# HGRN recurrence and a capacity-limited mixture of experts on one core: the second product of an expert in one matmul per chunk, one block of zeros moved, the scatters re-spaced

## The chip, the cores and the metric

The kernel runs on one core of a Trainium2 chip. The metric is the device time of one launch in microseconds (us), as the median of three runs. All times "at" some moment are counted from the start of the profiled span.

## What is computed

First a recurrence over time is run on 4 sequences of 5056 steps with 256 channels each; its output, 20224 rows of 256 numbers, goes into a router with 8 experts. An expert keeps at most 80 rows, those with the highest gate weight, and every other row of the output is zero.

```python
sig = 1 / (1 + exp(-f_logit))
f = lower_bound + (1 - lower_bound) * sig
for t in range(S):                      # S = 5056, h is (4, 256)
    h = f[:, t] * h + (1 - f[:, t]) * x[:, t]
    y[:, t] = h
...
expert = argmax(x @ w_gate)             # x is y as 20224 rows of 256
for e in range(8):                      # capacity 80 rows
    hid = maximum(x[tok] @ w1[e], 0)    # 256 -> 1024
    out[tok] = gate[tok, None] * (hid @ w2[e])   # 1024 -> 256
```

Everything is float32. The inputs of the recurrence are 41 MB, the weights of the experts 17 MB, the output 21 MB.

## The kernel before, in words

The kernel has three stages.

**Load stage.** A unit is 512 time steps of one sequence; there are 40. For each unit `load` brings in `f_logit` and `x` (512 KB each), ScalarE and GpSimd form the gate and the input, TensorE turns both so that time lies along the free axis (L251, L259), VectorE scans (L276), and TensorE computes the router's logits (L289). SyncE issues all loads on one queue, in program order. The output's zeros are written on the same queue, in blocks of 512 KB: `copied` (L137) copies a block that is already zero from one place of the output to another, `clear` (L151) writes one from a tile of zeros. One block goes out after every fourth unit's loads.

**Selection.** A short stage of VectorE, TensorE and GpSimd work picks the rows of each expert. In it the first 7 halves of weights and 22 blocks of zeros are put in the queue.

**Expert stage** (`experts`). Weights come in 32 halves of 512 KB, numbered 0 to 31 in the order of `halves_of`: both halves of `w1` of expert 0, then for each expert e both halves of `w1[e+1]` and both halves of `w2[e]`. They live in a ring of 7 slots, so half k is issued when half k - 7 has been used up. `more` issues two halves, and behind half k as many `copied` blocks as the tuple `BETWEEN` names k. Halves 20 and 21 are `w2` of expert 4, 24 and 25 of expert 5, 30 and 31 of expert 7; the last half is loaded in two pieces.

For expert e, `gather` copies its 80 columns one by one out of `h_all` (24 by VectorE, 32 by ScalarE, 24 by GpSimd), and `scaled` multiplies them. `hidden` computes the first product: 32 matmuls with 64 columns of weights each, two of them side by side in the array, 80 columns moving. `relu` turns it into `hid`, the first four chunks by ScalarE, the other four by VectorE. `result` computes the second product: for each of 8 chunks of 128 hidden units, `hid` is the stationary operand and 256 columns of `w2` move. A chunk is done as two matmuls, for slots 0 to 63 and for slots 64 to 79:

```python
H = P // 2
...
for c in range(FC):
    for s0, n in ((0, H), (H, K - H)):
        marks[e, c] = nc.tensor.matmul(
            y[ds(s0, n)], hid[:, c, ds(s0, n)], halves[c // CH][:, c % CH],
```

`finish` multiplies by the gates on VectorE, and `scatter` sends the 80 rows to the output with one indirect DMA from GpSimd's queue. TensorE's order is hidden(0), hidden(1), result(0), hidden(2), result(1), and so on to hidden(7), result(6), result(7). The scatters stand behind the gathers in GpSimd's program; `apart` names for a scatter the matmul (expert, chunk) whose end it waits for; the last scatter waits for all others to land.

Of the kernel before, what the change touches and what calls it, by code (L numbers as in the profile page):

```python
# [26 lines left out]
def kernel(  # L27
# [11 lines left out]
    nc = tc.nc  # L39
    B, S, D = x.shape  # L40
    E, _, F = w1.shape
    N = B * S
    DC = D // P
    FC = F // P
# [5 lines left out]
    K = (capacity + TOP - 1) // TOP * TOP  # L50
# [20 lines left out]
    FH, CH = F // 2, FC // 2  # L71
# [13 lines left out]
    def slot(i, name):  # L85
        return ring[i].tile([P, R * D], F32, name=name, tag="buf")
# [44 lines left out]
    def copied():  # L131

        at = written[0]
        n = min(P * ZH, TOTAL - at)
        if n:
            z = 2 * ZH if n % (2 * ZH) == 0 else D
            nc.sync.dma_start(out=out_flat[ds(at, n)].rearrange("(p k) -> p k", k=z),  # L137
                              in_=out_flat[:n].rearrange("(p k) -> p k", k=z))
            written[0] += n

    def clear(source):

        n = source.shape[1]
        at = written[0]
        if at >= TOTAL:
            return
        rows = min(P, (TOTAL - at) // n)
        if rows == 0:
            rows, n = 1, TOTAL - at
        dst = out_flat[ds(at, rows * n)].rearrange("(p k) -> p k", p=rows)  # L150
        nc.sync.dma_start(out=dst, in_=source[:rows, :n])  # L151
        written[0] += rows * n
# [9 lines left out]
    with tc.tile_pool(name="gsm", bufs=1) as gsm:  # L162
# [49 lines left out]
        def small_loads():  # L212

            nc.sync.dma_start(out=small[:, :E * P],
                              in_=w_gate.rearrange("(o p) e -> o (p e)", p=P))
            nc.sync.dma_start(out=small[:, E * P:], in_=lower_bound.rearrange("(o p) -> o p", p=P))

        def small_turned():
            turn = plt.tile([P, E + 1, DC], F32, name="small_t", tag="lt")
            for e in range(E + 1):  # L220
                row = small[:, e:E * P:E] if e < E else small[:, E * P:]
                nc.tensor.transpose(turn[:, e], row, ident[:DC, :DC])
            nc.vector.tensor_scalar(nomlb, turn[:, E], 1.0, -1.0, ALU.mult, ALU.add)
            nc.vector.tensor_scalar(omlb, turn[:, E], -1.0, 1.0, ALU.mult, ALU.add)
            return turn
# [158 lines left out]
        def unit(f, m):  # L384
            if 0 <= m < n_unit:
                f(m)
# [11 lines left out]
        TURN = LAST * B  # L398
# [3 lines left out]
        with tc.tile_pool(name="plg", bufs=1, space=PSUM) as plg, \  # L402
             tc.tile_pool(name="plt", bufs=1, space=PSUM) as plt:
            with tc.tile_pool(name="pss", bufs=2, space=PSUM) as pss, \
                 tc.tile_pool(name="psu", bufs=3, space=PSUM) as psu:
                for n in range(-AHEAD, n_unit):
                    unit(load, n + AHEAD)
                    m = n + AHEAD
                    if m == 1:
                        small_loads()  # L410
                    if m == 3:
                        clear(early)
                    elif 3 < m < TURN and m % 4 == 3:
                        copied()
                    elif m == n_unit - 1:
                        for _ in range(3):
                            copied()
                    unit(gate, n + 2)
                    if n == -2:
                        turn = small_turned()  # L420
                    if n == -1:
                        scaled_gate(turn)
                    unit(enter, n + 2)
                    unit(turn_s, n + 1)
                    unit(turn_u, n + 1)
                    if n == n_unit - 2:
                        zbuf = slot(0, "zbuf")
                        nc.gpsimd.memset(zbuf, 0.0)
                        exponentials(0, LAST - 1)
                    unit(decay, n + 1)  # L430
                    unit(scan, n)
                    if n > 1 and n % B == 1:
                        aside(n // B - 1)
                    if n == n_unit - 3:
                        assert len(jobs) == 4
                    some_of(1 if n < TURN or n >= n_unit - 3 else 2 if n < n_unit - 1 else 0)
                    if n == n_unit - 2:
                        exponentials(LAST - 1, LAST)
                        summed(0, 4)
                        valued(0, 4, nc.gpsimd)  # L440
                    unit(logits, n - 1)
                    if n > 0 and n % B == 0:
                        g = n // B - 1
                        jobs.append(lambda g=g: by_token(g))
                        if g % 2 or g >= LAST - 1:
                            g0 = g - 1 if g < LAST - 1 else g
                            jobs += [lambda g0=g0, g=g: shifted(g0, g + 1),
                                     lambda g0=g0, g=g: equals(g0, g + 1),
                                     lambda g0=g0, g=g: choice(
                                         g0, g + 1, nc.gpsimd if g < LAST - 1 else nc.vector)]  # L450
            with tc.tile_pool(name="pct", bufs=4, space=PSUM) as pct:
# [32 lines left out]
                c = turn((6, LAST - 1), (LAST - 1, LAST))  # L484
# [38 lines left out]

    w_sb = {}
    RANKING = 12
    BETWEEN = (7, 8, 8, 10, 12, 13, 15, 16, 18)
    for k, key in enumerate(halves_of[:NSLOT - 1]):
        w_sb[key] = half(*key)
        copied()
# [68 lines left out]
    with tc.tile_pool(name="sel", bufs=1) as sel, \  # L598
# [17 lines left out]
        for r in (rivals2, rivals):  # L616
            nc.tensor.matmul(r, mates, spread.rearrange("p c k -> p (c k)"),
                             start=True, stop=True)
# [89 lines left out]
    def experts(again):  # L708
        with tc.tile_pool(name="xp", bufs=3) as xp, \
# [7 lines left out]
            sent, marks = [], {}  # L717
# [16 lines left out]
            H = P // 2  # L734
# [22 lines left out]
            def result(e):  # L757
                halves = [w.pop((2, e, i)) for i in range(2)]
                hid = HID.pop(e)
                y = Y[e] = psy.tile([K, D], F32, name="y_ps", tag="y_ps")  # L760
                for c in range(FC):
                    for s0, n in ((0, H), (H, K - H)):
                        marks[e, c] = nc.tensor.matmul(  # L763
                            y[ds(s0, n)], hid[:, c, ds(s0, n)], halves[c // CH][:, c % CH],
                            start=c == 0, stop=c == FC - 1, skip_group_check=True)

            def finish(e):
                if e == 0:
# [4 lines left out]
            def scatter(e, behind=None):  # L773

                sent.append(nc.gpsimd.indirect_dma_start(  # L775
                    out=out, out_offset=bass.IndirectOffsetOnAxis(ap=goal[:, ds(e, 1)], axis=0),
                    in_=rows.pop(e), in_offset=None, bounds_check=N - 1, oob_is_err=False))
                if behind:
                    tc.add_manual_dep(sent[-1].ins, marks[behind].ins.name, mybir.DependencyInfo(
                        mybir.DependencyClass.Sync, mybir.DependencyReason.DATA), reason="apart")  # L780
                for other in sent[:-1]:
                    if e < E - 1:
                        tc.declare_no_dep(sent[-1].ins, other.ins, reason="other rows")
                    else:
                        tc.add_manual_dep(sent[-1].ins, other.ins.name, mybir.DependencyInfo(
                            mybir.DependencyClass.Sync, mybir.DependencyReason.DATA),
                            reason="all rows")

            def more(m):
                for _ in range(2 * m):  # L790
                    if late:
# [3 lines left out]
                        if not again:  # L795
                            for _ in range(BETWEEN.count(k)):
                                copied()
# [13 lines left out]
            if not again:  # L811
                busy(psy, 3, "y_ps")

            apart = {2: (E - 3, FC - 1), 3: (E - 2, 0), 4: (E - 2, FC - 1), 5: (E - 1, 1),
                     6: (E - 1, FC - 2)}
            for e in range(E):
                relu(e, ps)
                if e == 0 and not again:
                    gates_of(slots[:, 1])
                if e + 1 < E:  # L820
                    ps = hidden(e + 1)
                    more(1)
                if e == E - 4:
                    scatter(0)
                if e + 3 < E:
                    gather(e + 3)
                    scaled(e + 3)
                if e == E - 4:
                    scatter(1)
                result(e)  # L830
                more(1)
                finish(e)
                if e == 0 and not again:
                    found = consts.tile([1, 1], F32, name="found")
                    nc.vector.tensor_reduce(found, total, AX.X, ALU.add)
                    nc.vector.tensor_copy(doubt, found)
                    rows_of(consts, slots[:, 0], slots[:, 1])
            for e in range(2, E):
                scatter(e, apart.get(e))

    experts(False)
    assert written[0] == TOTAL, written

# [88 lines left out]
```

## Time and profile before

| | |
|---|---|
| median of 3 runs | 252.69 us (252.64 to 252.92) |
| the profiled execution | 253.41 us |
| its span, first to last instruction | 251.5 us |
| TensorE busy | 221.4 us (88%) |
| VectorE / ScalarE / GpSimd busy | 156.8 / 133.1 / 143.2 us |
| bytes moved by DMA | 80.61 MB |
| second product (L763), matmul records and busy time | 256, 71.3 us |

A float32 matmul leaves two matmul records and two weight-load records in the profile, one pair for each of its two passes. Such records overlap, so a record's own duration is not what it costs; the distance from one start to the next is. Weight loads have rows of their own (PEld). A DMA's time "to landing" runs from its issue until its semaphore has its full count.

### The profile page before, as it was taken

Reading aid. Unit: us, or ns where it says so; the run is one execution under the profiler, and the core shown is the slowest. Engines: PE = TensorE matmul, PEld = TensorE weight load, DVE = VectorE, ACT = ScalarE, POOL = GpSimd, SP = SyncE. Lnnn points to the kernel's source line nnn. Section 1 sums busy time; section 2 is a strip of 40 time slices with the busy share of each in tenths; the row PEclk is TensorE's granted clock in tenths of the full one; section 3 lists DMA queues with packets and bytes.
Section 4 is the critical chain, followed back from the end, with each engine's and each line's share of the span. In section 5 each row is a group of like instructions: output and inputs, shape, how many; then the busy total and the mean of one; then the engine's idle time right before and its main releaser. Section 6 shows DMA issues by size and latency. Waiting matters only on the chain.

```text
span 251.5 us, 6853 instructions
## 1 busy us (share of the span) xinstructions
PE 221.4 (88%) x2223; PEld 141.9 (56%) x2223; DVE 156.8 (62%) x400; ACT 133.1 (53%) x419; POOL 143.2 (57%) x287
## 2 busy tenths in 40 slices
PE   0699899899989998999966899799999999999960
PEld 0698787778868787777834646252525344352210
DVE  4189699999999999899999567435415051010100
ACT  4488798779787886888826066755042300000000
POOL 4678797889788798779844067650450620011211
PEclk9999999999999999999997979999999999999996
DMA  6999999999999999999999999969985474620000
GB/s 248 377 410 449 371 425 412 418 420 401 412 405 408 397 434 391 395 403 412 400 363 417 416 444 402 417 257 345 340 300 199 154 250 137 219 95 14 26 20 17
DMA packets 21363, 80.61 MB, mean 320 GB/s; under 512 B 2580, under 2 KB 2710, under 8 KB 20888
## 3 DMA queue, kind: packets, MB, share of 16 engines
q1 hardware_dynamic: 20936, 79.45, 80.4%
q0 software_dynamic: 384, 0.66, 0.9%
q8 instruction: 19, 0.31, 0.5%
q14 instruction: 24, 0.20, 0.2%
HBM read 72.62 MB, written 21.36 MB: 374 GB/s over the span
## 4 chain that ended last, share of the span: by engine, by line
PE 45%; issue 19%; ACT 10%; DVE 9%; DMA 9%; POOL 4%; ACTq 1%; DVEq 0%; POOLq 0%; SPq 0%
PE y_ps L763 14%; PE sp L251 11%; PE up L259 9%; PE lg L289 6%; DMA x_t<-in_x_dram 5%; ACT h_all L268 4%; ACT xe L727 3%; PE h_ps L747 3%; DMA f_t<-in_f_logit_dram 3%; DVE h_all L276 3%; POOL out_dram L775 2%; PE lt L313 2%; POOL x_t L245 2%; ACT ls L298 2%; DMA out_dram<-y,goal 1%
## 5 line engine op out<-in xcount | busy, mean ns | idle before, releaser
L245 POOL TENSOR_TENSOR x_t<-f_t,x_t 128x1024 f32<-128x1024 f32 x40 | 94.7, 2370 | 21.1 <-DMA x_t<-in_x_dram 10.6
L276 DVE TENSOR_TENSOR_SCAN h_all<-h_all,up 128x512 f32<-128x512 f32 (+1 forms) x80 | 95.8, 1244 | 9.9 <-PE up L259 6.4
L763 PE MATMUL y_ps<-w_sb,hid 128*64 128x256 f32 (+1 forms) x256 | 71.3, 393 | 1.4 <-ACT hid L754 1.4
L268 ACT ACTIVATE h_all<-sp,nomlb 128x512 f32<-128x512 f32 (+1 forms) x80 | 50.3, 677 | 16.5 <-PE sp L251 15.7
L763 PEld LDWEIGHTS y_ps<-w_sb,hid 128*64 128x64 f32 (+1 forms) x256 | 19.4, 115 | 50.4 <-issue 48.8
L241 ACT ACTIVATE f_t<-f_t 128x1024 f32<-128x1024 f32 x40 | 42.3, 1058 | 9.8 <-DMA f_t<-in_f_logit_dram 7.3
L259 PE MATMUL up<-ident,x_t 128*128 128x128 f32 x320 | 44.0, 278 | 2.8 <-DVE h_all L276 2.2
L251 PE MATMUL sp<-ident,f_t 128*128 128x128 f32 x320 | 45.4, 287 | 0.0
L251 PEld LDWEIGHTS sp<-ident,f_t 128*128 128x128 f32 x320 | 35.9, 145 | 7.8 <-issue 7.1
L259 PEld LDWEIGHTS up<-ident,x_t 128*128 128x128 f32 x320 | 36.7, 143 | 5.1 <-DVE h_all L276 3.7
L771 DVE TENSOR_SCALAR y<-y_ps,gates 80x256 f32<-80x256 f32 x8 | 3.8, 480 | 57.0 <-PE y_ps L763 51.5
L727 ACT COPY xe<-h_all 128x2 f32 x256 | 25.4, 190 | 18.8 <-issue 12.2
L727 POOL COPY xe<-h_all 128x2 f32 x192 | 24.3, 189 | 14.2 <-issue 7.0
L727 DVE COPY xe<-h_all 128x2 f32 x192 | 22.7, 173 | 12.0 <-issue 7.4
L775 POOL DMA_INDIRECT out_dram<-y,goal x8 | 7.5, 942 | 35.3 <-PE y_ps L763 31.1
L289 PE MATMUL lg<-h_all,wg 128*32 128x128 f32 (+1 forms) x640 | 26.4, 282 | 0.6 <-ACT ls L298 0.6
L754 ACT ACTIVATE hid<-h_ps 128x320 f32<-128x320 f32 x8 | 3.5, 435 | 39.2 <-PE h_ps L747 21.3
L747 PEld LDWEIGHTS h_ps<-xe,w_sb 128*64 128x64 f32 x512 | 18.2, 138 | 4.1 <-issue 3.6
L747 PE MATMUL h_ps<-xe,w_sb 128*64 128x80 f32 x512 | 19.5, 234 | 0.0
L289 PEld LDWEIGHTS lg<-h_all,wg 128*32 128x32 f32 x640 | 15.4, 108 | 7.0 <-issue 4.9
L731 POOL TENSOR_TENSOR xe<-xe,omlb 128x160 f32<-128x160 f32 x8 | 3.6, 452 | 23.5 <-DVE xe L727 22.1
L160 PE MATMUL warm<-h_all,ident 128*128 128x512 f32 x22 | 13.1, 740 | 0.0
(128 smaller groups left out, 105.6 us busy)
## 6 DMA issues: line engine op xcount, KB each, us to landing
f_t<-in_f_logit_dram SPq DMA_DIRECT2D x40, 512.0 KB, 6.6
x_t<-in_x_dram SPq DMA_DIRECT2D x40, 512.0 KB, 6.9
w_sb<-in_moe_w_dram SPq DMA_DIRECT2D x31, 512.0 KB, 5.0
out_dram<-out_dram SPq DMA_DIRECT2D x26, 512.0 KB, 8.2
out_dram<-zbuf SPq DMA_DIRECT2D x12, 512.0 KB, 10.0
out_dram<-h_all SPq DMA_DIRECT2D x1, 512.0 KB, 8.2
w_sb<-in_moe_w_dram SPq DMA_DIRECT2D x2, 256.0 KB, 2.8
out_dram<-out_dram SPq DMA_DIRECT2D x1, 256.0 KB
```

Source lines behind the costliest of these rows:

```text
L160: nc.tensor.matmul(warm, ident, h_all[:, 0, :4 * P], start=True, stop=True)
L241: nc.scalar.activation(s_t, s_t, ACT.Sigmoid, scale=-1.0)
L245: nc.gpsimd.tensor_tensor(u_t, sts[n], u_t, ALU.mult)
L251: nc.tensor.transpose(ps[:, ds(r * P, P)], sts[n][:, r, ds(o * P, P)], ident)
L259: nc.tensor.transpose(ps[:, r::R], uts[n][:, r, ds(o * P, P)], ident)
L268: nc.scalar.activation(columns(n, o).rearrange("p (k r) -> p k r", r=R), sps.pop((n, o)).rearrange("p (r k) -> p k r", r=R)[:, P - run(n / ...
L276: nc.vector.tensor_tensor_scan(h, h, ups.pop((n, o)), h_all[:, o, ds(spot(n - B) + G - 1, 1)] if n >= B else 0.0, ALU.mult, ALU.add)
L289: nc.tensor.matmul(lgs[g][ds(q * LC, LC), b, :k].rearrange("p (m i) -> p m i", i=2), wg[:, o], pairs[:, :, q], start=o == 0, stop=o == DC ...
L727: copy(X[e][:, :, ds(k + j, 1)], h_all[:, :, ds(v, 1)])
L747: nc.tensor.matmul(ps[i][ds(s * H, H), c], wo[o][:, at:at + J * (H - 1) + 1:J], xt[:, o], start=o == 0 and c == 0, stop=o == DC - 1, skip_ ...
L763: marks[e, c] = nc.tensor.matmul(y[ds(s0, n)], hid[:, c, ds(s0, n)], halves[c // CH][:, c % CH], start=c == 0, stop=c == FC - 1, skip_grou ...
L775: sent.append(nc.gpsimd.indirect_dma_start(out=out, out_offset=bass.IndirectOffsetOnAxis(ap=goal[:, ds(e, 1)], axis=0), in_=rows.pop(e), i ...
```

## The change

The second product is one matmul per chunk, with all 80 slots as the stationary operand. The block of zeros behind the loads of unit 35 is left out, and `BETWEEN` has ten places instead of nine, with later numbers. The first scatter is issued behind the last gather instead of ahead of it; scatter 1 joins the loop at the end; and `apart` names other matmuls.

```diff
@@ -410,7 +410,7 @@
                         small_loads()
                     if m == 3:
                         clear(early)
-                    elif 3 < m < TURN and m % 4 == 3:
+                    elif 3 < m < TURN - 1 and m % 4 == 3:
                         copied()
                     elif m == n_unit - 1:
                         for _ in range(3):
@@ -523,7 +523,7 @@
 
     w_sb = {}
     RANKING = 12
-    BETWEEN = (7, 8, 8, 10, 12, 13, 15, 16, 18)
+    BETWEEN = (7, 8, 8, 9, 10, 12, 14, 17, 19, 21)
     for k, key in enumerate(halves_of[:NSLOT - 1]):
         w_sb[key] = half(*key)
         copied()
@@ -759,10 +759,9 @@
                 hid = HID.pop(e)
                 y = Y[e] = psy.tile([K, D], F32, name="y_ps", tag="y_ps")
                 for c in range(FC):
-                    for s0, n in ((0, H), (H, K - H)):
-                        marks[e, c] = nc.tensor.matmul(
-                            y[ds(s0, n)], hid[:, c, ds(s0, n)], halves[c // CH][:, c % CH],
-                            start=c == 0, stop=c == FC - 1, skip_group_check=True)
+                    marks[e, c] = nc.tensor.matmul(
+                        y, hid[:, c], halves[c // CH][:, c % CH],
+                        start=c == 0, stop=c == FC - 1, skip_group_check=True)
 
             def finish(e):
                 if e == 0:
@@ -811,8 +810,8 @@
             if not again:
                 busy(psy, 3, "y_ps")
 
-            apart = {2: (E - 3, FC - 1), 3: (E - 2, 0), 4: (E - 2, FC - 1), 5: (E - 1, 1),
-                     6: (E - 1, FC - 2)}
+            apart = {1: (E - 3, FC - 1), 2: (E - 2, 0), 3: (E - 2, CH), 4: (E - 2, FC - 1),
+                     5: (E - 1, 2), 6: (E - 1, FC - 2)}
             for e in range(E):
                 relu(e, ps)
                 if e == 0 and not again:
@@ -820,13 +819,11 @@
                 if e + 1 < E:
                     ps = hidden(e + 1)
                     more(1)
-                if e == E - 4:
-                    scatter(0)
                 if e + 3 < E:
                     gather(e + 3)
                     scaled(e + 3)
                 if e == E - 4:
-                    scatter(1)
+                    scatter(0)
                 result(e)
                 more(1)
                 finish(e)
@@ -835,7 +832,7 @@
                     nc.vector.tensor_reduce(found, total, AX.X, ALU.add)
                     nc.vector.tensor_copy(doubt, found)
                     rows_of(consts, slots[:, 0], slots[:, 1])
-            for e in range(2, E):
+            for e in range(1, E):
                 scatter(e, apart.get(e))
 
     experts(False)
```

On TensorE, in the expert stage, the rows before, from the first product of expert 1 (`h_ps`) into the second product of expert 0 (`y_ps`); the last two columns are stationary and moving columns:

```order
L747 MATMUL h_ps<-xe,w_sb 64x80 x32
L763 MATMUL y_ps<-w_sb,hid 64x256
L763 MATMUL y_ps<-w_sb,hid 16x256
L763 MATMUL y_ps<-w_sb,hid 64x256
L763 MATMUL y_ps<-w_sb,hid 16x256
```

and the same place of the change, on to the next expert:

```order
L747 MATMUL h_ps<-xe,w_sb 64x80 x32
L762 MATMUL y_ps<-w_sb,hid 80x256 x8
L747 MATMUL h_ps<-xe,w_sb 64x80 x32
L762 MATMUL y_ps<-w_sb,hid 80x256 x8
L747 MATMUL h_ps<-xe,w_sb 64x80 x32
```

Sixteen matmuls of an expert, alternating between 64 and 16 columns, have become eight of 80.

On SyncE's queue, in the expert stage before, from half 13 (`w2` of expert 2, its second) to half 21 (L514 is a half of `w1`, L520 a half of `w2`, L137 a block of zeros, the last one of 256 KB):

```order
L520 DMA w_sb<-in_moe_w_dram 128x2x512
L137 DMA out_dram<-out_dram 16x8192
L514 DMA w_sb<-in_moe_w_dram 128x1024 x2
L137 DMA out_dram<-out_dram 16x8192
L520 DMA w_sb<-in_moe_w_dram 128x2x512
L137 DMA out_dram<-out_dram 16x8192
L520 DMA w_sb<-in_moe_w_dram 128x2x512
L514 DMA w_sb<-in_moe_w_dram 128x1024
L137 DMA out_dram<-out_dram 16x4096
L514 DMA w_sb<-in_moe_w_dram 128x1024
L520 DMA w_sb<-in_moe_w_dram 128x2x512 x2
```

and of the change, from half 13 to half 23:

```order
L520 DMA w_sb<-in_moe_w_dram 128x2x512
L514 DMA w_sb<-in_moe_w_dram 128x1024
L137 DMA out_dram<-out_dram 16x8192
L514 DMA w_sb<-in_moe_w_dram 128x1024
L520 DMA w_sb<-in_moe_w_dram 128x2x512 x2
L137 DMA out_dram<-out_dram 16x8192
L514 DMA w_sb<-in_moe_w_dram 128x1024 x2
L137 DMA out_dram<-out_dram 16x8192
L520 DMA w_sb<-in_moe_w_dram 128x2x512 x2
L137 DMA out_dram<-out_dram 16x4096
L514 DMA w_sb<-in_moe_w_dram 128x1024 x2
```

The last block of zeros stood behind half 18 and stands behind half 21.

## Rows read from the trace of the kernel before

**Rows 1.** The page's slices (40, of 6.29 us each): DMA rate; then all bytes.
```profile
GB/s 248 377 410 449 371 425 412 418 420 401 412 405 408 397 434 391 395 403 412 400 363 417 416 444 402 417 257 345 340 300 199 154 250 137 219 95 14 26 20 17
DMA packets 21363, 80.61 MB, mean 320 GB/s; under 512 B 2580, under 2 KB 2710, under 8 KB 20888
```

**Rows 2.** Windows: PE, PEld, DVE, ACT, POOL busy (instructions); clock, DMA share, GB/s.
```profile
5.00:25.00 20.00, 16.70 (x157) 15.25 (x161) 12.49 (x15) 14.01 (x19) 14.44 (x7) 1.00 1.04 410
...
145.00:163.00 18.00, 16.57 (x159) 8.54 (x158) 11.54 (x95) 12.48 (x127) 13.12 (x96) 0.92 1.03 419
163.00:190.00 27.00, 27.00 (x219) 10.81 (x220) 9.63 (x67) 11.04 (x103) 10.39 (x76) 1.00 0.82 300
190.00:222.00 32.00, 32.00 (x281) 13.38 (x278) 7.96 (x54) 4.54 (x35) 5.95 (x28) 1.00 0.59 203
```

**Rows 3.** TensorE in order of time, expert stage: start, duration, instruction.
```profile
158.49 0.43 PE L763 MATMUL y_ps<-w_sb,hid 128*64 128x256 f32 x1 [1.43 <-ACT hid L754]
...
189.61 2.44 PE L747 MATMUL h_ps<-xe,w_sb 128*64 128x80 f32 x64
191.87 8.91 PE L763 MATMUL y_ps<-w_sb,hid 128*64 128x256 f32 x32
200.72 2.44 PE L747 MATMUL h_ps<-xe,w_sb 128*64 128x80 f32 x64
...
225.21 17.80 PE L763 MATMUL y_ps<-w_sb,hid 128*64 128x256 f32 x64
```

**Rows 4.** SyncE's queue: what issues waited for; us in total, times, longest.
```profile
SPq L520 <- PE y_ps L763: 23.4, 6, 4.0
SPq L514 <- PE y_ps L763: 18.1, 5, 4.5
```

**Rows 5.** TensorE's weight loads in order of time, within one second product.
```profile
192.40 0.11 PEld L763 LDWEIGHTS y_ps<-w_sb,hid 128*16 128x16 f32 x2 [0.39 <-issue]
192.93 0.19 PEld L763 LDWEIGHTS y_ps<-w_sb,hid 128*64 128x64 f32 x2 [0.42 <-issue]
193.51 0.11 PEld L763 LDWEIGHTS y_ps<-w_sb,hid 128*16 128x16 f32 x2 [0.38 <-issue]
```

**Rows 6.** The chain of waits in the load stage: eight transposes of one unit.
```profile
77.44 0.87 PE up L259 x8
```

**Rows 7.** Weight loads of these transposes, by shape: busy us, mean ns, idle before.
```profile
L259 PEld LDWEIGHTS up<-ident,x_t 128*128 128x128 f32 x320 | 36.7, 143 | 5.1 <-DVE h_all L276 3.7 <-POOL x_t L245 1.3
```

**Rows 8.** All DMA from 0 to 163 us.
```profile
DMA packets 16026, 65.43 MB, mean 401 GB/s; under 512 B 1980, under 2 KB 1982, under 8 KB 15666
```

**Rows 9.** The scatters' queue, from 163 us: packets, MB, share of 16 engines.
```profile
q0 software_dynamic: 384, 0.66, 2.5%
```

**Rows 10.** DMA issues of weights, 192 to 222 us: median us to landing.
```profile
w_sb<-in_moe_w_dram SPq DMA_DIRECT2D x9, 512.0 KB, 3.3
```

**Rows 11.** The same, 145 to 163 us.
```profile
w_sb<-in_moe_w_dram SPq DMA_DIRECT2D x5, 512.0 KB, 9.3
```

**Rows 12.** The chain of waits at the end: start, duration, what.
```profile
241.94 0.03 POOLq L775
...
242.18 3.13 DMA out_dram<-y,goal
```

**Rows 13.** ScalarE in order of time: two gathers, with a relu between.
```profile
160.03 3.34 ACT L727 COPY xe<-h_all 128x2 f32 x32 [1.59 <-issue]
...
165.36 3.12 ACT L727 COPY xe<-h_all 128x2 f32 x32 [1.67 <-issue]
```

**Rows 14.** VectorE in order of time: finish of expert 6, relu of expert 7.
```profile
234.16 0.48 DVE L771 TENSOR_SCALAR y<-y_ps,gates 80x256 f32<-80x256 f32 x1 [10.23 <-PE y_ps L763]
234.56 0.48 DVE L755 TENSOR_SCALAR hid<-h_ps 128x320 f32<-128x320 f32 x1
```

**Rows 15.** TensorE in order of time, where its clock fell.
```profile
134.00 1.22 PE L617 MATMUL rivals<-spread,mates 128*128 128x192 f32 x3 [2.65 <-DVE spread L611]
```

**Rows 16.** The window behind it, columns as in rows 2.
```profile
134.10:137.40 3.30, 3.30 (x7) 2.23 (x8) 3.26 (x8) 2.33 (x9) 1.88 (x8) 0.50 1.03 421
```

## The prediction

> **What bounds the kernel now.** I read the page's slices first. From the second slice to the 26th (6 to 163 us) DMA moves 363 to 449 GB/s, and then the rate falls off [rows 1]. The windows say the same by stage: 410 GB/s early in the loads, 419 from 145 to 163 us with all sixteen DMA engines busy, then 300 and 203 [rows 2]. What ends where DMA slackens is seen in the same windows: from 163 us TensorE is busy for 27.00 us of 27 and 32.00 of 32. So there are two regimes: the queue is full until about 160 us, and from the first second product, at 158.49 us, TensorE sets the time. SyncE's queue shows who waits: loads of weights wait 23.4 and 18.1 us in total for a second product to give a ring slot free [rows 4].
>
> TensorE's order of time gives its beat. A first product starts at 189.61 us, the second product behind it at 191.87, the next first product at 200.72 [rows 3]: 2.27 us and 8.85 us. Eight of the one and six of the other are 84.4 us, from 158.49 to 242.9, and the last row of the group shows no gap between the last two second products.
>
> A chunk of a second product costs 8.85 / 8 = 1.106 us, and the weight loads show how: they come in twos for 16 columns and for 64 in turn, at 192.40, 192.93 and 193.51 us [rows 5]. So the two matmuls of a chunk run one behind the other, 0.53 to 0.58 us each.
>
> **The one wide matmul.** The nearest row for a full-width stream is eight transposes, each of 128 moving columns in one pass, in 0.87 us: 0.85 ns a column, with a load of 143 ns for other weights behind each, hidden [rows 6, 7]. A float32 matmul has two passes, so 256 columns cost 2 x 256 x 0.85 = 0.436 us. The narrow matmuls fit this: 0.436 of each is streaming, and (1.106 - 0.872) / 2 = 0.117 us goes at each change of width. Below 0.436 the chunk cannot come, as streaming alone takes that. Above, I bound it by today's cost of one narrow matmul, 0.553 us (a load stays exposed once per chunk), and at the far end by a load of 143 ns exposed on both passes, 0.72 us. I take 0.436, since the loads hidden in [rows 6, 7] are wider than 80 columns and change each time. A second product then costs 3.49 us instead of 8.85, and at 0.553 it costs 4.42. Between a first and a second product the width still changes, so I put 0.12 us at each of 12 such places. TensorE alone would need 8 x 3.49 + 6 x 2.27 + 12 x 0.12 = 42.9 us, and end at 201.4.
>
> Here a rule speaks against the change. The Trainium skill ("TensorEngine Tiling (Array Packing)", Key Properties) says that different tiles run weight loads and matmuls in parallel; by it the 64 and the 16 columns share the array already, a chunk costs 0.43 us now, and nothing is saved. The first product does so: 64 records of 80 columns would take 4.35 us at 0.85 ns a column, and take 2.27 [rows 3]. The second product does not: 32 records of 256 columns would take 6.96 us one by one, and take 8.85. I go by the row.
>
> **What is late next: DMA.** With TensorE that fast the queue stays full. Slots come free early: half 11, the first that waited for a second product, needs half 4 used up at 158.49 + 1.75 = 160.2 us, while a half then takes 9.3 us from issue to landing because of the queue ahead of it [rows 11]. The limit is therefore bytes. All DMA is 80.61 MB [rows 1], 0.66 of it scatters [rows 9], leaving 79.95; 65.43 are moved by 163 us [rows 8]. Behind half 20, the first that expert 4's second product needs, stand eleven halves (5.77 MB) and half a block of zeros (0.26). So 79.95 - 5.77 - 0.26 - 65.43 = 8.49 MB are left for it at 163 us; at 410 GB/s they are 20.7 us, to 183.7. A lone half lands 3.3 us after its issue [rows 10], of which 1.28 is its bytes, so I add 2.0: 185.7 us.
>
> From there TensorE runs four second products, two first ones and four changes of width: 13.96 + 4.54 + 0.47 = 19.0 us, to 204.7. The other gates lie behind: half 24 lands at 163 + (79.95 - 3.67 - 65.43) / 0.41 + 2.0 = 191.5 us and is wanted at 191.7; the last piece lands at 200.4 and is wanted at 203.8. The gathers don't bind: ScalarE starts one every 5.33 us [rows 13], against about 6 us per expert here. Nor does VectorE between the last two second products: its finish and relu take 0.9 us [rows 14], and the relu is wanted only by the fifth chunk, 1.75 us on.
>
> **The moved zeros.** The block dropped at unit 35 is 1.28 us of a full queue, and comes back between late halves. As every block still stands ahead of half 22, and the queue is full to there, it is worth nothing; if the queue had spare time late, it would be worth up to 1.28 us, and if the late blocks delayed a half that TensorE waits for alone, it would cost as much. The last block now stands behind half 21, so it lands near 187 us, and scatter 0 must wait for that; behind scatter 0 in GpSimd's queue are only scatters.
>
> **Scatters.** Putting scatter 0 behind gather 7 takes some 1 us of GpSimd out of the way of a gather that has time. Scatter 1 gains a wait for the end of second product 5; queued behind it are scatters 2 to 7 alone. By the beat above their matmuls end at about 194.8, 198, 199.8, 201.2, 202.5 and 204.2 us, at least 1.3 apart, and each holds GpSimd's queue for about 1.2 (0.27 until it starts, 0.91 busy). So they don't pile up, and the end hangs as now on scatter 6: its matmul, the seventh chunk of the last product, ends by 241.94, it lands at 242.18 + 3.13, and the last scatter follows [rows 12]; from 241.94 to the span's end, 251.5, are 9.6 us.
>
> **Sum.** 204.7 - 0.44 (one chunk) + 9.6 = 213.8 us of span. The profiled execution took 253.41 for a span of 251.5, so 1.9 more: 215.7. It lay 0.7 above the median of the runs; **215.0 us**.
>
> **Rivals.**
> A load stays exposed (chunk 0.553): TensorE alone binds, 158.49 + 8 x 4.42 + 15.0 = 208.9, which gives 219.1 us. For it: [rows 5] show loads that hide nothing. Against: there the width changes each time. At the far bound, 0.72, it is 230.
> The queue does not stay full: halves are issued only as slots come free, and DMA goes at the 300 GB/s of 163 to 190 us [rows 2]. Half 20 then lands at 163 + 28.3 + 2.0 = 193.3, and the time is 222.6. Against: slots free some 6 us ahead of need.
> DMA is quicker or the dropped block counts: TensorE alone, 1.28 us earlier, ends at 200.1 and the time is 210.5.
> Nothing saved: the two narrow matmuls share the array as the first product's pairs do, what is lost lies elsewhere, and the wide one costs what the pair does: 252.7 us. Loads 0.53 to 0.58 us apart [rows 5] leave it little. The tiling rule above is this rival.
> Slower: the clock. TensorE's clock stood at half (1.2 of 2.4 GHz) from 134.1 us, after 2.65 us without work [rows 15, 16]. If waits for DMA brought it down for the whole expert stage, all streaming doubles: 85.8 us from 158.49, to 244.3, and 254.2 us in the end. It decides only if nearly the whole stage runs low, since at full clock the work is half. Against: in the load stage TensorE also waits in between (16.70 of 20 busy) at clock 1.00 [rows 2]; here it would be busy nine tenths.
>
> **Numbers.** Forecast 0.70 (its own range 211.5 to 218.5: rate 400 to 419 GB/s, the 2.0 us of landing); exposed load 0.12, of which 0.02 beyond 223; queue not full 0.09; quicker 0.03; nothing saved 0.03; slower 0.03. The range 211 to 223 leaves out the last two, the far bound and the edges. Against 0.2%, about what a measurement of this kernel can tell from no change: faster 0.94, same 0.03, slower 0.03.
>
> **What would show it.** Right: second products of 16 records, about 3.5 us apart from the next start; DMA near 410 GB/s to about 195 us; waits of TensorE for weights at halves 16 to 24; scatters 1 us apart or more at the end, with the last landing some 9.6 us behind the seventh chunk. Wrong: second products above 4.4 us (loads exposed); a DMA rate that falls before 190 us; a clock below 1.00 after 160 us; scatters that wait for each other, or gathers that TensorE waits for.

## The result and the profile after

The changed kernel takes 217.41 us (median of 4 runs, 216.56 to 218.05), the kernel before 252.81 (4 runs): 0.8595 of the time, with a 95% interval of 0.856 to 0.8629. Forecast were 215.0 us and a range of 211 to 223. The profiled execution took 217.71 us for a span of 215.9. One execution further down, 223.34 us, stood in a slower state of the chip and is left out of its kernel's ratio.

The page's slices first: 40 of 5.40 us each, DMA rate.

```profile
GB/s 221 419 362 407 404 420 427 406 424 415 430 370 415 420 405 406 417 406 408 369 394 391 348 390 408 415 441 435 393 420 390 432 411 408 400 389 368 74 53 20
```

The rate holds to the 37th slice, some 200 us, where that of before fell off after 163 us [rows 1]. The windows say the same by stage (columns as in rows 2):

```profile
163.00:190.00 27.00, 22.25 (x285) 16.55 (x282) 15.62 (x112) 14.54 (x133) 14.48 (x101) 1.00 1.02 407
190.00:200.00 10.00, 10.00 (x153) 7.83 (x152) 1.75 (x4) 0.88 (x2) 2.04 (x2) 1.00 1.00 370
```

From 163 to 190 us DMA is fully busy at 407 GB/s and TensorE has 4.75 us without work; in [rows 2] it was the other way round. SyncE's queue agrees: its waits for a second product to free a slot fell from 23.4 and 18.1 us [rows 4] to

```profile
SPq L520 <- PE y_ps L762: 3.3, 3, 1.4
...
SPq L514 <- PE y_ps L762: 2.0, 1, 2.0
```

TensorE in order of time, expert stage (as rows 3):

```profile
158.10 3.68 PE L762 MATMUL y_ps<-w_sb,hid 128*80 128x256 f32 x16 [1.47 <-ACT hid L754]
161.71 2.44 PE L747 MATMUL h_ps<-xe,w_sb 128*64 128x80 f32 x64
164.08 3.68 PE L762 MATMUL y_ps<-w_sb,hid 128*80 128x256 f32 x16
168.21 1.33 PE L747 MATMUL h_ps<-xe,w_sb 128*64 128x80 f32 x32 [0.45 <-DMA w_sb<-in_moe_w_dram]
170.77 1.33 PE L747 MATMUL h_ps<-xe,w_sb 128*64 128x80 f32 x32 [1.23 <-DMA w_sb<-in_moe_w_dram]
...
187.76 3.65 PE L762 MATMUL y_ps<-w_sb,hid 128*80 128x256 f32 x16 [1.55 <-DMA w_sb<-in_moe_w_dram]
191.34 2.44 PE L747 MATMUL h_ps<-xe,w_sb 128*64 128x80 f32 x64
193.71 3.68 PE L762 MATMUL y_ps<-w_sb,hid 128*80 128x256 f32 x16
197.32 2.44 PE L747 MATMUL h_ps<-xe,w_sb 128*64 128x80 f32 x64
199.69 7.13 PE L762 MATMUL y_ps<-w_sb,hid 128*80 128x256 f32 x32
```

Sixteen records stand where 32 stood; from the start of a second product to the start of the next first one are 3.6 us in place of 8.85 [rows 3]. The last wait for weights ends at 187.76, at expert 4's second product, whose weights are halves 20 and 21. Behind it nothing waits for DMA any more.

GpSimd at the end (start, busy, idle before): scatters 1 to 7.

```profile
197.68 0.91 POOL L774 DMA_INDIRECT out_dram<-y,goal  x1 [6.05 <-PE y_ps L762]
200.63 0.91 POOL L774 DMA_INDIRECT out_dram<-y,goal  x1 [2.04 <-PE y_ps L762]
202.36 0.92 POOL L774 DMA_INDIRECT out_dram<-y,goal  x1 [0.81 <-PE y_ps L762]
203.66 0.91 POOL L774 DMA_INDIRECT out_dram<-y,goal  x1 [0.38 <-PE y_ps L762]
204.95 0.91 POOL L774 DMA_INDIRECT out_dram<-y,goal  x1 [0.38 <-PE y_ps L762]
206.68 0.91 POOL L774 DMA_INDIRECT out_dram<-y,goal  x1 [0.81 <-PE y_ps L762]
210.54 0.91 POOL L774 DMA_INDIRECT out_dram<-y,goal  x1 [2.95 <-DVEq L843]
```

Each waits for its matmul and none for the scatter ahead of it, except the last, which waits for all as before.

### The profile page after: what moved, and what is told of

Read it like the earlier page. It is cut to its first block, busy times and chain, and to the rows that moved or that the text cites. A ratio compares the mean times of both kernels' runs of the same rounds, so it can differ in the third digit from the quotient of the medians.

```text
span 215.9 us, 6597 instructions
## 1 busy us (share of the span) xinstructions
PE 180.7 (84%) x2095; PEld 141.4 (65%) x2095; DVE 156.7 (73%) x400; ACT 132.7 (61%) x419; POOL 143.6 (66%) x287
## 4 chain that ended last, share of the span: by engine, by line
DMA 41%; PE 35%; issue 8%; ACT 7%; POOL 4%; DVE 2%; SPq 0%; POOLq 0%; DVEq 0%; ACTq 0%
PE sp L251 13%; DMA w_sb<-in_moe_w_dram 12%; DMA out_dram<-out_dram 10%; PE up L259 10%; DMA out_dram<-zbuf 9%; PE lg L289 7%; DMA f_t<-in_f_logit_dram 6%; ACT h_all L268 4%; POOL out_dram L774 3%; PE lt L313 3%; DMA x_t<-in_x_dram 2%; ACT ls L298 2%; DVE h_all L276 2%; PE y_ps L762 2%; DMA out_dram<-y,goal 1%
## 5 line engine op out<-in xcount | busy, mean ns | idle before, releaser
L727 POOL COPY xe<-h_all 128x2 f32 x192 | 24.5, 189 | 15.1 <-issue 7.8
L762 PE MATMUL y_ps<-w_sb,hid 128*80 128x256 f32 x128 | 29.3, 382 | 3.9 <-DMA w_sb<-in_moe_w_dram 2.4
L762 PEld LDWEIGHTS y_ps<-w_sb,hid 128*80 128x80 f32 x128 | 18.5, 150 | 12.5 <-ACT hid L754 1.8
L747 PE MATMUL h_ps<-xe,w_sb 128*64 128x80 f32 x512 | 20.0, 235 | 2.3 <-DMA w_sb<-in_moe_w_dram 2.2
L160 PE MATMUL warm<-h_all,ident 128*128 128x512 f32 x22 | 13.7, 769 | 0.0
L313 PE MATMUL lt<-ident,ls 128*128 128x128 f32 (+1 forms) x40 | 7.4, 308 | 4.8 <-ACT ls L298 4.8
```

Source lines behind the costliest of these rows:

```text
L313: nc.tensor.transpose(lts[g0][:k, g - g0, j], ls[:, j::R], ident)
L727: copy(X[e][:, :, ds(k + j, 1)], h_all[:, :, ds(v, 1)])
L747: nc.tensor.matmul(ps[i][ds(s * H, H), c], wo[o][:, at:at + J * (H - 1) + 1:J], xt[:, o], start=o == 0 and c == 0, stop=o == DC - 1, skip_ ...
L762: marks[e, c] = nc.tensor.matmul(y, hid[:, c], halves[c // CH][:, c % CH], start=c == 0, stop=c == FC - 1, skip_group_check=True)
```

## Experiments

The kernel before ran again beside each group of experiments, with medians from 253.39 to 254.49 us (252.81 in the result). Kernels of different groups are therefore compared by their ratio to it first; a difference of 1 us between two medians is less than what separates these groups.

**The wide matmul alone, and the moves alone.** The first kernel is the one before with only this edit; the second is the changed kernel with the edit undone.

```diff
-    for s0, n in ((0, H), (H, K - H)):
-        marks[e, c] = nc.tensor.matmul(
-            y[ds(s0, n)], hid[:, c, ds(s0, n)], ...
+    marks[e, c] = nc.tensor.matmul(y, hid[:, c], ...
```

> The kernel before with the one wide matmul per chunk and nothing else of the change. Theory (the gain is the matmul; the bytes ahead of half 20 set the rest, and a moved block changes nothing while the queue is full): within 0.7% of the changed kernel's 217.4 us, 216 to 219. Rival (the moved blocks and re-spaced scatters carry a part of the gain): above 220.

> The changed kernel with the two narrow matmuls per chunk put back: only the block of zeros, BETWEEN and the scatters are changed. Theory: TensorE binds as before, 252 to 253.5 us. Rival (the dropped block gives the expert stage its start 1.28 us earlier): 251.4 or less.

The merge alone: 217.19 us (216.56 to 218.49, 6 runs), 0.8561 of before, interval 0.8521 to 0.8601. The moves alone: 253.44 (252.38 to 254.35, 12 runs), ratio 0.9987, interval 0.9959 to 1.0015. So the merge is the whole gain, and the moved zeros and scatters are worth nothing that these runs can tell from nothing, on the old beat or on the new one.

The merge alone in TensorE's order of time:

```profile
160.38 3.68 PE L762 MATMUL y_ps<-w_sb,hid 128*80 128x256 f32 x16 [0.83 <-ACT hid L754]
...
180.59 1.93 PE L762 MATMUL y_ps<-w_sb,hid 128*80 128x256 f32 x8 [1.75 <-DMA w_sb<-in_moe_w_dram]
182.96 1.93 PE L762 MATMUL y_ps<-w_sb,hid 128*80 128x256 f32 x8 [0.45 <-DMA w_sb<-in_moe_w_dram]
...
199.35 7.13 PE L762 MATMUL y_ps<-w_sb,hid 128*80 128x256 f32 x32
```

Its expert stage began 2.28 us later than that of the changed kernel, and its last products began 0.34 us earlier. TensorE had time to lose until DMA's next gate. More zeros stand early in this queue, so its last waits are at halves 16 and 17 and not at 20.

**Two matmuls of equal width.** Chunk by chunk two matmuls of 64 columns stand in place of the one of 80; the second is for slots 16 to 79, so rows 64 to 79 of its result belong to other slots.

```diff
+    for at, s0 in ((0, 0), (H, K - H)):
+        marks[e, c] = nc.tensor.matmul(
+            y_all[ds(at, H)], hid[:, c, ds(s0, H)], ...
```

> The changed kernel with each chunk of the second product as two matmuls of 64 columns each, for slots 0 to 63 and slots 16 to 79, beside each other in the array. Rows 64 to 79 of each expert's result then hold other slots than the reference's. Theory (what made the pair run one behind the other is the change between 64 and 16 columns): the two share the array, a chunk costs 0.44 us, and the time is 216 to 218.5. Rival (two matmuls of a second product never overlap, whatever their widths): 0.87 us a chunk, TensorE alone 158.1 + 8 x 6.98 + 6 x 2.27 = 227.6, some 238 us.

Measured: 216.45 us (215.33 to 216.94, 4 runs), 0.8511, interval 0.846 to 0.8561. TensorE in order of time:

```profile
187.26 3.67 PE L764 MATMUL y_ps<-w_sb,hid 128*64 128x256 f32 x32 [1.55 <-DMA w_sb<-in_moe_w_dram]
190.74 2.41 PE L747 MATMUL h_ps<-xe,w_sb 128*64 128x80 f32 x64
192.95 3.65 PE L764 MATMUL y_ps<-w_sb,hid 128*64 128x256 f32 x32
```

Thirty-two records take 3.67 us here and 8.91 in [rows 3]. Only the widths differ: 64 and 64 share the array, 64 and 16 go one behind the other. A second product starts 2.21 us after the first product here and 2.37 in the changed kernel, where the width changes in between; the next first product starts 3.48 us after it here and 3.58 there. So what the kernel before lost was neither columns nor matmuls but came from the unequal widths. No kernel ran two matmuls of 16 columns, so that it is the change, and not the width of 16 by itself, is argued. The Trainium skill ("TensorEngine Tiling (Array Packing)", Key Properties) has both halves of this: different tiles run in parallel, and changing the tiling mode drains TensorE. The trace agrees with the first for equal widths, and with the second at 0.10 to 0.16 us a change between 64 and 80.

**Bytes ahead of half 20.** Four kernels differ from the changed one in the late blocks of zeros alone: without any (that part of the output is left unwritten), with two blocks behind halves 22 and 24, with three blocks written a second time ahead of half 20, and with all ten later.

```diff
-    BETWEEN = (7, 8, 8, 9, 10, 12, 14, 17, 19, 21)
+    BETWEEN = ()                                     # none
+    BETWEEN = (7, 8, 8, 9, 10, 12, 14, 17, 22, 24)   # two later
+    BETWEEN = (8, 9, 10, 12, 14, 17, 20, 22, 24, 26) # all later
+    if k in (14, 17, 19): ...                        # three written twice
```

> The changed kernel without the ten blocks of zeros between late halves (BETWEEN empty); that part of the output is left unwritten. Theory (DMA's bytes hold back half 20 and with it the end; TensorE alone needs 8 x 3.6 + 6 x 2.37 = 43.0 us from 158.1): its last matmul ends near 201.1 instead of 206.8, and the time is 5.7 us shorter, 211.2 to 212.7. Rival (gathers, relu or exposed weight loads set the beat): within 1 us of 217.4.

> The changed kernel with the last two places of BETWEEN at 22 and 24 instead of 19 and 21: one block of zeros less ahead of half 20. Theory (bytes ahead of half 20 hold TensorE back, 1.28 us a block): half 20 lands near 186.4 us instead of 187.7, and the time is about 1.2 us shorter, 215.5 to 216.8. Rival (the gate lies elsewhere, or the later block delays a half that TensorE waits for as much): 217.4, within 0.4.

> The changed kernel with three blocks of zeros written once more, behind halves 14, 17 and 19, all ahead of half 20: 1.57 MB more. Theory (the queue is full, and every byte ahead of half 20 is on the path): 3 x 1.28 = 3.8 us longer, 220.5 to 222. Rival (DMA has time to spare there): under 219.

> The changed kernel with BETWEEN at 8, 9, 10, 12, 14, 17, 20, 22, 24, 26. Theory (the queue is full to half 31, so a later block only moves the gate from half 20 to a later half): half 20 lands 3.8 us earlier, half 28 as before at 198.5, and from there two second products of 3.6 us: last matmul near 205.6 instead of 206.8, 216.2 us, 215.5 to 217. Rival (the later zeros hold scatter 0 back and with it the end): above 217.5.

| late blocks | us (lowest to highest, runs) | ratio, 95% interval |
|---|---|---|
| none | 212.96 (211.03 to 213.70, 4) | 0.836, 0.8305 to 0.8416 |
| two later | 216.34 (215.79 to 217.08, 6) | 0.8534, 0.8502 to 0.8567 |
| all later | 216.26 (215.13 to 218.34, 6) | 0.8543, 0.8497 to 0.8588 |
| three more | 222.08 (221.89 to 224.34, 6) | 0.8784, 0.8742 to 0.8825 |

Without the blocks TensorE never waits for a weight (order of time):

```profile
141.66 4.16 PE L684 MATMUL slots<-what,put 128*80 128x8 bf16 x60
...
159.71 3.68 PE L762 MATMUL y_ps<-w_sb,hid 128*80 128x256 f32 x16 [0.84 <-ACT hid L754]
163.32 2.44 PE L747 MATMUL h_ps<-xe,w_sb 128*64 128x80 f32 x64
165.69 3.68 PE L762 MATMUL y_ps<-w_sb,hid 128*80 128x256 f32 x16
...
195.58 7.13 PE L762 MATMUL y_ps<-w_sb,hid 128*80 128x256 f32 x32
```

An expert takes 5.98 us, and six of them lead from 159.71 to 195.58. TensorE alone thus needs 43.0 us, to 202.71. The median of 212.96 lies just above the 211.2 to 212.7 expected: the stage began 1.6 us later than in the changed kernel, and the expectation had it begin at the same time. With two blocks later the wait at half 20 is gone and the last products start 1.97 us earlier:

```profile
185.29 3.65 PE L762 MATMUL y_ps<-w_sb,hid 128*80 128x256 f32 x16
...
197.72 7.13 PE L762 MATMUL y_ps<-w_sb,hid 128*80 128x256 f32 x32
```

Of these, 0.72 us stood already at the first second product (157.38 against 158.10), which leaves 1.25 for the block taken from ahead of half 20; 1.28 was expected. The medians differ by 1.07 us and the intervals overlap a little (0.8502 to 0.8567 and 0.856 to 0.8629), so the time alone would not show it. With three more, TensorE's order of time and SyncE's queue show

```profile
190.32 5.34 PE L762 MATMUL y_ps<-w_sb,hid 128*80 128x256 f32 x16 [2.71 <-DMA w_sb<-in_moe_w_dram]
```

```profile
SPq L799 <- DMA out_dram<-out_dram: 8.8, 2, 4.7
```

The time rose by 4.67 us, to just above the 220.5 to 222 expected, and not by the sum expected (3.84 us for 1.57 MB at 410 GB/s). The three extra blocks (L799) write the same place, so the second and the third waited for the one before, 8.8 us in all, and half 20 was issued at 184.15 instead of 177.41 us. Its second product started only 2.56 us later than in the changed kernel, and then took 1.69 us more, at a granted clock of 0.68 from 190.3 to 195.6 us. The run shows that work ahead of half 20 sets the end; a price per byte can't be read from it. All later gains no more than two later: TensorE's waits then stand at the halves behind (it starts again at 185.79 and 193.29 us).

**Scatters without distance.** The changed kernel keeps scatters 1 to 6 behind chosen matmuls. Three kernels take distances away:

```diff
-    apart = {1: (E - 3, FC - 1), 2: (E - 2, 0), 3: (E - 2, CH), ...
+    apart = {1: (E - 3, FC - 1)}                  # from scatter 2 on
+    apart = {1: (E - 3, FC - 1), 2: (E - 2, 0)}   # from scatter 3 on
+    apart = {1: (E - 2, 0)}                       # all behind first product 7
```

> The changed kernel with apart for scatter 1 alone: scatters 2 to 6 go as soon as their rows are finished, and scatter 6 about 2.5 us earlier than behind the seventh chunk of the last product. Theory (the end hangs on scatter 6, which the last scatter waits for to land; the 9.5 us behind the seventh chunk are 3 us of landing that can be ahead): the last scatter starts near 207.6 instead of 210.5 us, and the time is 2.5 to 3 us shorter, 214.4 to 215.2. Rival (scatters without distance hold each other up, or slow TensorE's weights): 217 or more.

Measured: 218.96 us (218.26 to 223.34, 6 runs), 0.8641, interval 0.8597 to 0.8686. I had expected 2 to 3 us of gain over the changed kernel, and there is none (0.8641 against 0.8595, with intervals that just overlap): the theory that the distances only cost time fell. The ratio is of the five runs up to 221.29 us (their median is 218.77). The profiled execution is the sixth, so the rows come from a second run of the same kernel.

> The changed kernel without distances from scatter 2 on, once more, since the profiled execution of its first run took 223.34 us, longer than all its others (218.26 to 221.29). Theory (scatters 1.22 us apart beside first product 7 hold TensorE up): 218 to 220 us, and gaps put down to issue in first product 7 or second product 6 again, 1 to 3 us in sum, with scatters 1 to 5 at 1.22 us from each other. Rival (the gaps belonged to that one execution; scatters merely land late): no gap, the last second products end by 207.5 us, and what is lost lies behind them.

Again no gain: 219.54 us (218.39 to 220.0, 5 runs), 0.8628, interval 0.8581 to 0.8675. TensorE in order of time, and GpSimd beside it:

```profile
197.07 2.15 PE L747 MATMUL h_ps<-xe,w_sb 128*64 128x80 f32 x54
199.50 0.38 PE L747 MATMUL h_ps<-xe,w_sb 128*64 128x80 f32 x4 [0.28 <-issue]
200.25 0.39 PE L747 MATMUL h_ps<-xe,w_sb 128*64 128x80 f32 x5 [0.37 <-issue]
201.71 0.23 PE L747 MATMUL h_ps<-xe,w_sb 128*64 128x80 f32 x1 [1.07 <-issue]
201.87 0.88 PE L762 MATMUL y_ps<-w_sb,hid 128*80 128x256 f32 x3
203.14 8.28 PE L762 MATMUL y_ps<-w_sb,hid 128*80 128x256 f32 x29 [0.40 <-issue]
```

```profile
197.42 0.91 POOL L774 DMA_INDIRECT out_dram<-y,goal  x1 [6.05 <-PE y_ps L762]
198.64 0.92 POOL L774 DMA_INDIRECT out_dram<-y,goal  x1 [0.31 <-issue]
...
208.76 0.92 POOL L774 DMA_INDIRECT out_dram<-y,goal  x1 [5.54 <-DVE y L770]
```

Scatters 1 to 5 run 1.22 us apart from 197.42. TensorE comes to the end of first product 7 and stops four times for "issue", 2.1 us in sum, with neither data nor a slot missing; then its clock falls (0.51 granted from 203.14 to 205.5 us). Its last product ends at 211.4 us, in the changed kernel at 206.8, so scatter 6 comes 2.1 us later.

Is it the bunch, or the bunch beside a first product?

> The changed kernel (217.41 us), with distances only for scatters 1 and 2. Beside the run without distances from scatter 2 on (218.96 us) it differs in the distance of scatter 2 alone, which keeps scatters 2 to 6 behind first product 7. Theory (only scatters beside the first product cost TensorE time): no gap put down to issue, scatters 2 to 6 at 1.22 us from each other from about 200.7 us, scatter 6 at about 205.5 in place of 206.7, and 216.0 to 217.0 us. Rival (scatters 1.22 us apart cost TensorE time in every product): gaps of 0.2 to 1.0 us in the last second products, and 218 us or more.

> The changed kernel with one distance alone: scatter 1 waits for the first column of second product 6, scatters 2 to 6 for nothing but their rows, so six scatters stand 1.22 us apart and none beside a first product. Theory (only beside the first product do they hold TensorE up): no gap put down to issue, scatter 1 at about 200.6 us of the span, scatters 2 to 6 at 201.9 to 206.7, as late as in the changed kernel, and 216.5 to 218 us. Rival (a bunch of this length holds TensorE up anyway): gaps of 0.2 us or more in the last second products, scatter 6 behind 207.5, and 218.5 us or more.

> The kernel with two blocks of zeros later (216.34 us), and distances only for scatters 1 and 2: scatter 2 still waits for the first column of second product 6, scatters 3 to 6 for nothing but their rows. Theory (scatters 1.22 us apart hold up TensorE only while a first product runs, and the last scatter waits for scatter 6 to land): scatter 2 at about 198.7 us of the span, 3 to 6 at 199.9, 201.1, 202.3 and 203.5, no gap put down to issue in the last two second products, scatter 6 lands at about 206.7 in place of 207.9, and the time is 214.8 to 215.6 us. Rival (scatters that close hold up TensorE whatever it runs): gaps of 0.2 to 1.0 us in the last second products, and 216.5 us or more.

With scatters 1 and 2 alone held back: 215.92 us (215.18 to 217.83, 6 runs; 216.0 to 217.0 was expected), 0.8525, interval 0.8478 to 0.8571. TensorE, then GpSimd:

```profile
196.70 2.44 PE L747 MATMUL h_ps<-xe,w_sb 128*64 128x80 f32 x64
199.06 7.13 PE L762 MATMUL y_ps<-w_sb,hid 128*80 128x256 f32 x32
```

```profile
200.00 0.91 POOL L774 DMA_INDIRECT out_dram<-y,goal  x1 [2.04 <-PE y_ps L762]
201.22 0.91 POOL L774 DMA_INDIRECT out_dram<-y,goal  x1 [0.30 <-issue]
...
204.88 0.91 POOL L774 DMA_INDIRECT out_dram<-y,goal  x1 [0.30 <-DMA out_dram<-y,goal]
208.29 0.91 POOL L774 DMA_INDIRECT out_dram<-y,goal  x1 [2.51 <-DVE y L770]
```

No gap, with scatters as close as before. With all six behind first product 7: 216.89 us (216.05 to 217.69, 5 runs), 0.8542, interval 0.8494 to 0.8591; again none:

```profile
197.19 2.44 PE L747 MATMUL h_ps<-xe,w_sb 128*64 128x80 f32 x64
199.56 7.13 PE L762 MATMUL y_ps<-w_sb,hid 128*80 128x256 f32 x32
```

The kernel without distances, run beside this one, took 218.39 to 220.0 us, so no run of the one reaches one of the other. Six scatters in a row cost TensorE nothing beside the second products; a row that runs across the end of first product 7 does. With two blocks later as well: 216.66 us (214.85 to 217.75, 6 runs), 0.8545, interval 0.8506 to 0.8584, against an expected 214.8 to 215.6. Its profiled execution, the 214.85, is as expected (scatter 6 at 203.88, the last at 207.42); the median is not and lies where the rival had it (216.5 or more), though without the rival's gaps. The run is inconclusive. The kernel with scatters 1 and 2 alone held back has the lowest median of those that write the whole output rightly, 1.5 us under the changed kernel. Its trace has the last scatter 2.25 us earlier than there, 0.62 of which stood already at half 20, but the intervals overlap (0.8478 to 0.8571 and 0.856 to 0.8629).

Why TensorE stops for issue stays open. In the run without distances one packet of the instruction queue q14 went through between 199.5 and 206 us, in the changed kernel and the two others shown three. That made me think of late code, but it isn't shown: with two blocks later there are two packets and no stop, and in the run without distances TensorE had gone on, at 203.14 us, before the next packet came at 206.34.

## Why the prediction was right, step by step

- **The wide matmul: right.** 3.65 us for a product of eight chunks that start 0.43 us apart fits the 0.436 taken from the transposes; the load of 80 columns is hidden, and the rival of an exposed load fell. So did "nothing saved", as a second product went from 8.85 to 3.6 us. The pair of 64s shows why the first product was no guide for that rival: equal widths do share the array. My reading of the rule was short there: I weighed only that tiles run in parallel. The time alone would not have told the forecast from the exposed load (219.1 us, also inside the range); the rows do.
- **What is late next: right.** DMA binds, as the changed kernel's windows show, and the runs without blocks and with two moved behind half 21 show that what stands ahead of half 20 sets the end. "Queue not full" (300 GB/s) fell to the 407 measured.
- **The landing of half 20: mis-sized by 2.0 us**, the only term that was. The step said 185.7; TensorE began on it at 187.76. Two pieces, from all DMA up to 163 and up to 184.3 us:

```profile
DMA packets 16009, 65.17 MB, mean 400 GB/s; under 512 B 1970, under 2 KB 1972, under 8 KB 15654
...
DMA packets 18471, 73.88 MB, mean 401 GB/s; under 512 B 2239, under 2 KB 2241, under 8 KB 18022
```

  By 163 us 0.26 MB less had moved than in [rows 8], 0.6 us at 410 GB/s. Half 20 needs 79.95 - 5.77 - 0.26 = 73.92 MB, reached at 184.4 us (forecast 183.7). From there to the start at 187.76 are 3.4 us, where I had added 2.0 from a lone half [rows 10]. The lone half was the wrong row. As the run stood, an earlier half 20 could have given back 1.55 us and no more: TensorE, held up by the waits before, was free for it only at 186.2.
- **19.0 us of TensorE from there: right.** 187.76 to 206.82 (199.69 + 7.13) is 19.06, with 0.10 to 0.16 at a change of width where 0.12 was taken: 2.37 us from a first product to the second, 2.21 where the widths are equal. TensorE alone, in the run without late blocks, took 43.0 us for a forecast of 42.9.
- **The tail, 9.6 us: right.** From the seventh chunk's end (206.82 - 0.43) to the span's end, 215.9, are 9.5.
- **Zeros and scatters worth nothing: right**, by the merge and the moves alone.
- **Gates for TensorE: partly wrong.** I named halves 16 to 24. The waits stand at 10, 11, 13, 15 and 20, none behind. As the last wait alone set the end here, the sum didn't feel it.
- **Sum:** 187.76 + 19.06 - 0.43 + 9.5 = 215.9 us of span; 1.8 around it make the 217.71 of the profiled run. Against 215.7 that is 2.0, half 20 alone; the other 0.4 of the 2.4 us between forecast and median is that I took 0.7 off for the median, where the profiled run lay 0.3 above it.

The slower rival, the clock, did not come here, yet the run with three more blocks shows its beginning: 2.71 us without work, then a granted clock of 0.68 on the mean of 190.3 to 195.6 us.

## What to carry to other kernels

Before you count columns, look whether neighbouring matmuls have the same width: 64 and 16 in turn ran one behind the other and lost more than half of each second product, and one matmul for both costs what one of them streams. When an engine becomes that much faster, ask how many bytes of the next bound stand ahead of the last piece it waits for; that gave the time within 2.4 us, and moving two blocks later, so that one less stood ahead of that piece, was worth 1.25 us in the trace and about as much in the medians, where the noise is as large. Price a landing from a transfer in a queue as full as the one you forecast: the loads of [rows 11] landed 2.2 to 2.6 us behind the bytes of their queue, where 2.0 was taken and 3.6 came by that count.

## What I had not expected of the hardware

- **Landing can lag far behind the bytes.** Summed over the packets of all queues, as above, everything up to half 20 had started some 3.4 us before TensorE could start; by SyncE's queue alone it is 3.6. By that queue alone it is 3.1 to 3.6 us for halves and blocks issued from 157 to 179 us, and 2.7 to 2.8 for weights issued from 191 to 194 us, when the queue was running empty. In the kernel before it is 2.2 to 2.7 for those issued from 141 to 157 us, with the queue as full; and 1.7 for half 20 of the run with three more blocks, where the queue had been held up. So a full queue alone doesn't set it, and what does stays open. The Trainium skill ("DMA: Bandwidth & Descriptors", Why a DMA increments its semaphore by 16 and not by 1) says that the semaphore is full only with the last engine's count, so one engine that is behind could do this; no run here shows which engine was late.
- **A row of scatters can stop TensorE's issue**, 2.1 us in four pieces, at one place of the program and not at another; why is open.
- **The clock in the selection sets when the expert stage starts.** The small matmuls `slots` took 4.16 us in the run without late blocks, at a granted clock of 0.50 (1.2 of 2.4 GHz) from 139.9 to 145.8 us; in the changed kernel they took

```profile
141.21 2.46 PE L684 MATMUL slots<-what,put 128*80 128x8 bf16 x60
```

  at 1.00. There the clock had stood at 0.64 from 134.3 to 139 us, during the matmuls that keep TensorE busy, and was back before the selection; in the other run these matmuls were through early, at full clock, and TensorE then had 2.09 us without work. The stage starts 1.9 us later for it: from the `rivals` matmuls to the first second product are 24.5 us in the changed kernel, and 26.4 in the run without late blocks and in the merge alone, where `slots` took 4.16 us too. Where DMA binds this is hidden, as in the merge alone; where TensorE binds it shows, and may be part of why the runs without late blocks spread from 211.03 to 213.70.
